# Reordering the fixed cycle of a fused attention and two-layer kernel: probabilities ahead of the scores, input matmuls in halves

## The chip, the cores and the metric

The kernel runs on one core of one Trainium2 chip. The metric is the device time of one execution in microseconds (us). Before the change three runs took 1663.9, 1669.32 and 1674.0 us, so the median is 1669.32 us. Every reading of the trace below comes from one profiled execution of 1669.26 us.

## The reference

Three stages follow each other. Attention with a top-32 mask comes first: 4 batches, 8 heads, 576 positions, head width 64. Its 2304 tokens of width 512 then go through two layers with 2048 hidden units each, the first with a rational function between its two products, the second with h cos(h).

```python
scores = scale * np.matmul(q, k.transpose(0, 1, 3, 2))
kth = np.partition(scores, -top_k, axis=-1)[..., -top_k:-top_k + 1]
scores = np.where(scores >= kth, scores, -1000000000.0)
attn = softmax(scores); x = attn @ v            # -> (2304, 512)
h = x @ w_in                                    # first layer
g = (a0 + a1*h + a2*h**2 + a3*h**3) / (1 + |b0|*|h| + |b1|*h**2 + 1e-6)
x = g @ w_out
h = x @ w_in2; g = h * cos(h); out = g @ w_out2 # second layer
```

## The kernel before

The three stages run as one pipeline. Its step is called a unit here; the loop at the end of `body` counts it as `u` and passes it to the functions as `i`. In unit i attention works on 128 query positions of a pair of heads: `topk` finds the 32 greatest scores of tile i, `av(i - 1)` transposes the probabilities of tile i-1 and multiplies them with V, and `qk(i + 1)` computes the scores of tile i+1. Beside it one group of 256 hidden units of each layer, for a block of 256 tokens, goes through its steps: the first layer runs 9 units behind attention (`UA`), the second 18 units (`UB`). There are 72 attention tiles, so a unit past 72 holds work of the layers alone.

Every fp32 product of the layers is made of three products of fp32r halves (a high and a low part). `mm_in` therefore issues 24 matmuls of 256 columns for one group (2 blocks of hidden units, 4 chunks of the width, 3 products) into one bank of PSUM, `out1` another 24, and `out2` 12 of 512 columns.

Units 20 to 71 (`U0`, `U1`) run in a fixed cycle. The function `unit` writes the order of the cycle by hand: the wrapper `InOrder` ties each instruction to the one written before it on the same engine, so VectorE (DVE), ScalarE (ACT), GpSimd (POOL) and TensorE (PE) each follow the order of `unit`. SyncE's queue, which starts the streamed loads, is placed by the framework. Outside those units `events` places the work of the layers, and the framework may reorder it.

The order of TensorE in one unit before the change is: nine transposes of the probabilities (tiles `pp..a`, `pp..b`, and one into `sx`), the scores of the first head (four matmuls into `sx`), all 24 matmuls of `in1`, the scores of the second head, the probabilities times V (18 matmuls into `sx`), 24 of `in2`, 12 of `out2`, 24 of `out1`.

ScalarE follows with: three copies of the transposes (`pt`), the copy `sS` of the first head's scores, the high part `gg` of the first layer, in every second unit a table load and the sine, then `w`, `r`, `q`, `u` of `in1`, the copy `sS` of the second head's scores, the copy `xs` of the attention output, in every second unit a table load, the high part `gg` of the second layer, `nb` and the two exponentials `e`, two steps `r` of the reciprocal, `hs`, `rr`, `n` of `in2`, and the high part `q` of a later query tile.

PSUM has eight banks. The tag `h` has two, which pass in turn to `pp..a`, `pp..b`, `h` of `in1`, (in every fourth unit `bc` of the normalisation) and `h` of `in2`. The tile `sx` has two, shared by the scores (columns 0 to 287 of both banks), one transpose and the attention output (columns 288 to 415 of one bank each). `y` and `o` have two each. The streamed low parts of the weights go through four buffers of the tag `st`, with five loads in each unit.

Of the kernel before, what the change touches and what calls it, by code (L numbers as in the profile page):

```python
# [36 lines left out]
NG = NF // 2  # L37
SINB = 2
UA, UB = 9, 18
# [76 lines left out]
def body(tc, out, qt, kt, vt, ident_d, w1_d, w1o_d, a_d, b_d, w2_d, w2o_d):  # L116
# [5 lines left out]
    with ExitStack() as ctx:  # L122
# [27 lines left out]
        nu = len(units)  # L150
# [35 lines left out]
        def high_q(i):  # L186
            if 8 <= i < nu:
                qs_[i][1] = x = att.tile([P, 2, 2, P], F32R, tag="q", bufs=QB, name=f"q{i}")
                A.activation(x[:, 0], qs_[i][0], AF.Copy)
# [287 lines left out]
        def mm_in(m, k, g):  # L477
            h = ps_h.tile([P, 2, BT], F32, tag="h", name=f"h{m}_{k}_{g}")
            xh, xl = xhl[k] if m == 0 else x2hl[k]
            lo = lot.pop((m, k, g)).rearrange("p f (c t) -> p f c t", t=P)  # L480
            for i in range(2):
                f = 2 * g + i
                for c in range(NCC):
                    wh = whi[m][:, c, f * P:(f + 1) * P]
                    PE.matmul(h[:, i, :], wh, xh[:, c, :], start=(c == 0), stop=False)
                    PE.matmul(h[:, i, :], wh, xl[:, c, :], start=False, stop=False)
                    PE.matmul(h[:, i, :], lo[:, i, c, :], xh[:, c, :], start=False, stop=(c == NCC - 1))
            return h

        g1, ys, x2hl = {}, {}, {}  # L490

        def in1(k, g):
            h = mm_in(0, k, g).rearrange("p a t -> p (a t)")
            w, q, r, u = (mo.tile([P, BT * 2], F32, tag="m1" + t, bufs=NU if t == "u" else N1, name=f"{t}{k}_{g}") for t in "wqru")
            A.activation(w, h, AF.Copy)
            A.activation(r, w, AF.Abs)
            A.activation(q, r, AF.Identity, scale=b1, bias=b0)
            A.activation(u, w, AF.Identity, scale=na3, bias=na2)
            g1[k, g] = (q, r, u, w)

        def pol1(k, g):
            q, r, u, w = g1[k, g]
# [43 lines left out]
        def x2high(k):  # L546
            x2hl[k] = [late[0].tile([P, NCC, BT], F32R, tag=t, name=f"{t}{k}") for t in ("x2h", "x2l")]
            for c in range(2):
                cs = slice(2 * c, 2 * c + 2)
                A.activation(x2hl[k][0][:, cs], ys[k][:, cs], AF.Copy)  # L550
# [6 lines left out]
        rt, rp, os_, g2 = {}, {}, {}, {}  # L557

        def in2(k, g):
            g2[k, g] = mm_in(1, k, g).rearrange("p a t -> p (a t)")  # L560

        def phase2(k, g):
            h = g2.pop((k, g))
            if g % SINB == 0:
                rp[k, g // SINB] = late[0].tile([P, SINB, 512], F32, tag="rr", bufs=2, name=f"rr{k}_{g}")
            rs = rp[k, g // SINB]
            rr = rs[:, g % SINB]
            hs = late[0].tile([P, 512], F32, tag="hs", bufs=N2, name=f"hs{k}_{g}")
            A.activation(hs, h, AF.Copy)
            n = late[0].tile([P, DM], F32, tag="n", bufs=OBB, name=f"n{k}_{g}")  # L570
            if k >= DV2:
                V.tensor_scalar(rr, hs, 1.0 / TWO_PI, 0.25, op0=ALU.mult, op1=ALU.add)
            else:
                A.activation(rr, hs, AF.Identity, scale=1.0 / TWO_PI, bias=quarter)
            A.activation(n, rr, AF.Identity, bias=magic)
            rt[k, g] = rr, hs, n
# [45 lines left out]
        def store(k, t):  # L622
            o, parts = os_[k], qts[2 * k + t]
            n = P // len(parts)
            if k == NB - 1:
                if t == 0:
                    rt["ob"] = late[0].tile([P, SINB, DM], F32, tag="rr", bufs=2, name=f"ob{k}")
                ob = rt["ob"][:, t]
                A.activation(ob[:, :DM // 2], o[:, t, :DM // 2], AF.Copy)
                V.tensor_copy(ob[:, DM // 2:], o[:, t, DM // 2:])  # L630
            else:
                ob = late[0].tile([P, DM], F32, tag="ob", bufs=OBB, name=f"ob{k}_{t}")
                A.activation(ob, o[:, t, :], AF.Copy)
            for c, (b, tt) in enumerate(parts):
                row = b * S + tt * P
                (SP if c == 0 else A).dma_start(out=out[row:row + n, :], in_=ob[c * n:(c + 1) * n, :])
# [12 lines left out]

        flat = []  # L650
        for u in range(UB + NB * NG + 3):
            for f, d in ((in1, UA), (in2, UB), (out2, UB + 3), (out1, UA + 1)):
                if 0 <= u - d < NB * NG:
                    flat.append((f, *divmod(u - d, NG)))
        loads = []
# [38 lines left out]
        def ev(x, *fs):  # L694
            if 0 <= x < NB * NG:
                for f in fs:
                    run_event((f, *divmod(x, NG)))

        def last(x):
            return 0 <= x < NB * NG and x % NG == NG - 1  # L700
# [6 lines left out]
        nrm, low, held, x2, ob = [], [], [], [], []  # L707
# [51 lines left out]
        def events(u, p):  # L759
            if p == 0:  # L760
                ev(u - UA - 1, *((mid1,) if u <= U0 else (mid1, end1)))
                ev(u - UB - 1, mid2, sin2, table)
            if p == 1:
                for k in x2:
                    x2low(k)
                for k, t in ob:
                    store(k, t)
                x2.clear()
                ob.clear()
                if u > U0:  # L770
                    ev(u - UB - 3, low2)
                    ev(u - UA - 1, low1)
                ev(u - UB - 2, mul2, high2)
                ev(u - UA, in1, pol1, rec1)
            if p == 2:
                if u < U0:
                    ev(u - UA - 1, end1, low1)
                ev(u - UB, in2, phase2)
            if p == 3:
                ev(u - UB - 3, out2)  # L780
                if last(u - UB - 3):
                    store((u - UB - 3) // NG, 0)
                    store((u - UB - 3) // NG, 1)
            if p == 4:
                ev(u - UA - 1, out1)
                if last(u - UA - 1):
                    x2high((u - UA - 1) // NG)
                    x2.append((u - UA - 1) // NG)

        def unit(i, prev):  # L790
            t = topk(i)
            next(t)
            next(prev)
            next(prev)
            for x in low:
                next(x, None)
            low.clear()
            a = av(i - 1)
            next(a)
            nq = qk(i + 1) if i + 1 < nu else iter(())  # L800
            next(nq, None)
            ev(i - UA - 1, mid1, end1)
            low_q(i + 2, V)
            if i % 4 == 0:
                nrm.append(norm((i - 1) // 8, (i - 1) // 4 % 2))
                next(nrm[-1])
            ev(i - UB - 1, mid2)
            for k in x2:
                x2low(k)
            x2.clear()  # L810
            ev(i - UB - 3, low2)
            ev(i - UA - 1, low1)
            for k, h in ob:
                store(k, h)
            ob.clear()
            ev(i - UB - 1, sin2)
            ev(i - UB - 2, mul2)
            ev(i - UA, in1, pol1)
            next(nq, None)
            if i + 2 < nu:  # L820
                load_k(i + 2)
            load_q(i + 4)
            if i % 4 == 0:
                next(nrm[-1])
            next(a, None)
            load_v(i)
            if i % 4 == 0:
                next(nrm[-1])
            ev(i - UB - 1, table)
            ev(i - UB - 2, high2)  # L830
            ev(i - UB, in2)
            ev(i - UB - 3, out2)
            ev(i - UA - 1, out1)
            for _ in range(4):
                next(t)
            ev(i - UA, rec1)
            ev(i - UB, phase2)
            high_q(i + 3)
            if i % 8 == 0:
                for x in nrm:  # L840
                    next(x)
                low.extend(nrm)
                nrm.clear()
            if last(i - UA - 1):
                x2high((i - UA - 1) // NG)
                x2.append((i - UA - 1) // NG)
            if last(i - UB - 3):
                store((i - UB - 3) // NG, 0)
                ob.append(((i - UB - 3) // NG, 1))
            for x, a in held:  # L850
                store_k(x, *a)
            held[:] = [(prep(*a), a) for a in preps.get(i, [])]
            return t
# [64 lines left out]
```

## Time and profile before

| what | value |
|---|---|
| median of three runs | 1669.32 us |
| profiled execution | 1669.26 us, its span 1667.5 us |
| PE busy | 1339.2 us (80%) |
| DVE busy | 1204.0 us (72%) |
| ACT busy | 1114.5 us (67%) |
| POOL busy | 587.2 us (35%) |
| mean granted clock of PE | 0.886 |

The span is the time from the first to the last instruction in the trace, and the execution's own time holds what lies around it. Busy shares are means over stages with different limits. PE's busy time counts matmuls that overlap in the array, so it does not say how many more could be done. A granted clock of 1.00 is 2.4 GHz, 0.50 is 1.2 GHz. Nearly all instructions are recorded under line 80, the wrapper's call, so groups are read by their tiles' names.

### The profile page before, as it was taken

The page shows a single profiled execution, that of the slowest core. Times are in us where ns is not written, and L with a number is a line of the kernel's source. Part 1 is how long each engine was busy: PE and PEld are TensorE (multiplying, and loading weights), DVE is VectorE, ACT ScalarE, POOL GpSimd, SP SyncE. Part 2 cuts the span into 40 slices and gives each one's busy share as a digit, 9 for nine tenths or more (in the row PEclk, how much of TensorE's full clock was granted, in tenths as well). Part 3 has the DMA queues.
Part 4 walks back from the last instruction along what each step waited for, and adds up shares of the span by engine and source line. Part 5 has one row for each costly group of instructions (what it writes and reads, how often), then busy time and mean ns, then how long its engine had stood idle before and what let it go on. Part 6 is the DMA issues. An engine that isn't in the chain of part 4 may idle for free.

```text
span 1667.5 us, 25031 instructions
## 1 busy us (share of the span) xinstructions
PE 1339.2 (80%) x8944; PEld 1181.9 (71%) x8944; DVE 1204.0 (72%) x2514; ACT 1114.5 (67%) x1918; POOL 587.2 (35%) x434
## 2 busy tenths in 40 slices
PE   6776866677878888788878887888887888899998
PEld 3344655577777777777777777777777777789986
DVE  7989978897767766767777677676776576746643
ACT  7787778566676666666666666666666665668753
POOL 3665555323333333333333333333333333332000
PEclk9677887788898989889898999898988898899999
DMA  8977688523455544444555544444445555556776
GB/s 272 324 239 239 210 260 290 167 80 130 162 176 174 185 163 150 145 154 162 166 176 189 169 155 155 167 154 145 151 161 175 190 200 201 187 184 228 244 253 223
DMA packets 155948, 314.98 MB, mean 189 GB/s; under 512 B 12592, under 2 KB 47536, under 8 KB 155824
## 3 DMA queue, kind: packets, MB, share of 16 engines
q1 hardware_dynamic: 122832, 261.99, 46.7%
q10 hardware_dynamic: 32992, 51.39, 9.6%
q8 instruction: 71, 1.16, 0.3%
q14 instruction: 53, 0.43, 0.1%
HBM read 278.20 MB, written 35.13 MB: 188 GB/s over the span
## 4 chain that ended last, share of the span: by engine, by line
PE 47%; ACT 23%; DVE 15%; DMA 6%; issue 4%; ACTq 2%; POOL 2%; SPq 0%; POOLq 0%; DVEq 0%
PE h L80 18%; PE sx L80 10%; PE o L80 9%; PE y L80 8%; DVE e L80 6%; DVE hd L80 4%; ACT sS L80 3%; ACT r L80 3%; ACT rr L80 2%; ACTq L80 2%; ACT L80 2%; ACT u L80 2%; DVE cb L80 2%; ACT e L80 2%; ACT w L80 2%
## 5 line engine op out<-in xcount | busy, mean ns | idle before, releaser
L80 DVE MAX8 hd<-e 128x8 f32<-128x288 f32 (+1 forms) x576 | 320.6, 596 | 0.0
L80 DVE TENSOR_TENSOR e<-sS 128x576 f32<-128x576 f32 x144 | 169.9, 1219 | 158.1 <-ACT sS L80 148.0
L80 DVE MATCH_REPLACE8 e<-hd,e 128x288 f32<-128x288 f32 (+1 forms) x432 | 230.9, 541 | 0.0
L80 PE MATMUL y<-gg,w1o 128*128 128x256 f32 x1152 | 217.1, 287 | 11.5 <-DVE x2l L80 6.6
L80 POOL TENSOR_TENSOR gg<-rr,gg 128x512 fp32r<-128x512 f32 x56 | 73.2, 1308 | 418.4 <-DVE rr L80 314.7
L80 DVE SCALAR_TENSOR_TENSOR e<-sS,hd,e 128x576 f32<-128x576 f32 x144 | 122.1, 877 | 131.8 <-ACT e L80 131.8
L80 PE MATMUL o<-w2o,gg 128*128 128x512 f32 x864 | 211.2, 392 | 3.3 <-DMA w2o<-w2o 3.2
L80 PEld LDWEIGHTS y<-gg,w1o 128*128 128x128 f32 x1152 | 186.8, 194 | 19.6 <-ACT gg L80 10.9
L80 PE MATMUL h<-x2h,w2hi 128*128 128x256 f32 x576 | 196.8, 342 | 0.5 <-ACT hs L80 0.5
L80 PE MATMUL h<-x2l,w2hi 128*128 128x256 f32 x576 | 186.4, 324 | 0.0
L80 PE MATMUL h<-x2h,lo 128*128 128x256 f32 x576 | 184.2, 320 | 1.4 <-DMA lo<-w2lo 1.4
L80 PEld LDWEIGHTS o<-w2o,gg 128*128 128x128 f32 x864 | 157.1, 188 | 35.5 <-DMA w2o<-w2o 4.9
L80 PE MATMUL h<-xh,w1hi 128*128 128x256 f32 x576 | 167.9, 291 | 0.8 <-ACT pt17a L80 0.3
L80 PE MATMUL h<-xl,w1hi 128*128 128x256 f32 x576 | 166.3, 289 | 0.0
L80 PE MATMUL h<-xh,lo 128*128 128x256 f32 x576 | 166.2, 289 | 0.0
L80 PE MATMUL y<-gg,w1ol 128*128 128x256 f32 x576 | 164.2, 285 | 0.2 <-DMA w1ol<-w1ol 0.2
L80 PE MATMUL sx<-k,q 128*128 128x288 f32 (+1 forms) x576 | 108.2, 316 | 55.5 <-ACT xs L80 10.3
L80 POOL TENSOR_TENSOR gg<-u,gg 128x512 fp32r<-128x512 f32 x64 | 83.8, 1309 | 191.1 <-ACT gg L80 191.1
L80 PEld LDWEIGHTS h<-x2h,w2hi 128*128 128x128 f32 x576 | 137.0, 238 | 15.9 <-issue 14.2
L80 PEld LDWEIGHTS h<-x2l,w2hi 128*128 128x128 f32 x576 | 137.2, 238 | 0.2
L80 PEld LDWEIGHTS h<-x2h,lo 128*128 128x128 f32 x576 | 134.8, 234 | 2.1 <-DMA lo<-w2lo 2.0
L80 PEld LDWEIGHTS sx<-k,q 128*128 128x128 f32 (+1 forms) x576 | 83.9, 190 | 71.0 <-ACT xs L80 11.5
(1023 smaller groups left out, 3456.5 us busy)
## 6 DMA issues: line engine op xcount, KB each, us to landing
w2o<-w2o SPq DMA_DIRECT2D x144, 512.0 KB, 4.5
lo<-w1lo SPq DMA_DIRECT2D x72, 512.0 KB, 3.7
w1ol<-w1ol SPq DMA_DIRECT2D x72, 512.0 KB, 3.7
lo<-w2lo SPq DMA_DIRECT2D x72, 512.0 KB, 4.5
k<-kdr ACTq DMA_DIRECT2D x44, 576.0 KB, 4.9
raw<-w SPq DMA_DIRECT2D x32, 512.0 KB, 5.1
v<-vt ACTq DMA_DIRECT2D x48, 320.0 KB, 3.1
qr<-qt ACTq DMA_DIRECT2D x72, 128.0 KB, 3.7
```

Of the source, the lines that this page charges most:

```text
L80: r = f(*a, **k)
```

## The change

The change rewrites the order inside `unit`, with the same instructions and the same tiles. It has these parts.

- `mm_in` issues 12 of its 24 matmuls at once and returns a function for the other 12; `in1` and `in2` become `in1`/`in1b` and `in2`/`in2b`.
- TensorE's order becomes: transposes, first half of `in1`, probabilities times V, second half of `in1`, scores of the first head, first half of `in2`, scores of the second head, second half of `in2`, `out1`, `out2`.
- ScalarE's order becomes: `pt` three times, `gg` of the first layer, sine, `xs`, `w`, `r`, `sS` of the first head, `q`, `u`, `sS` of the second head, the issues of the loads of k, q and v, table load, `gg` of the second layer, and the rest as before.
- `out1` goes before `out2` everywhere, also in the list from which the streamed loads are issued and in `events`.
- The rest of a normalisation that lay ahead of `mid1` and `end1` on VectorE goes behind them; both stores of a finished output block move into the unit after it.

```diff
-            for i in range(2):
+
+            def half(i):
                 f = 2 * g + i
                 for c in range(NCC):
...
-            return h
+
+            half(0)
+            return h.rearrange("p a t -> p (a t)"), half
...
-            for f, d in ((in1, UA), (in2, UB), (out2, UB + 3), (out1, UA + 1)):
+            for f, d in ((in1, UA), (in2, UB), (out1, UA + 1), (out2, UB + 3)):
...
         def unit(i, prev):
             t = topk(i)
             next(t)
             next(prev)
             next(prev)
+            a = av(i - 1)
+            next(a)
+            ev(i - UA - 1, mid1, end1)
             for x in low:
                 next(x, None)
             low.clear()
-            a = av(i - 1)
-            next(a)
-            nq = qk(i + 1) if i + 1 < nu else iter(())
-            next(nq, None)
-            ev(i - UA - 1, mid1, end1)
...
-            for k, h in ob:
-                store(k, h)
+            for k in ob:
+                store(k, 0)
+            ev(i - UB - 1, sin2)
+            ev(i - UA, in1)
+            next(a, None)
+            if i % 4 == 0:
+                next(nrm[-1])
+            ev(i - UB - 2, mul2)
+            if i % 4 == 0:
+                next(nrm[-1])
+            ev(i - UA, in1b, copy1)
+            nq = qk(i + 1) if i + 1 < nu else iter(())
+            next(nq, None)
+            ev(i - UA, lin1, pol1)
+            ev(i - UB, in2)
+            next(nq, None)
+            ev(i - UB, in2b)
+            for k in ob:
+                store(k, 1)
             ob.clear()
-            ev(i - UB - 1, sin2)
-            ev(i - UB - 2, mul2)
-            ev(i - UA, in1, pol1)
-            next(nq, None)
             if i + 2 < nu:
                 load_k(i + 2)
             load_q(i + 4)
-            if i % 4 == 0:
-                next(nrm[-1])
-            next(a, None)
             load_v(i)
-            if i % 4 == 0:
-                next(nrm[-1])
+            ev(i - UA - 1, out1)
+            ev(i - UB - 3, out2)
             ev(i - UB - 1, table)
             ev(i - UB - 2, high2)
-            ev(i - UB, in2)
-            ev(i - UB - 3, out2)
-            ev(i - UA - 1, out1)
             for _ in range(4):
                 next(t)
             ev(i - UA, rec1)
-            ev(i - UB, phase2)
-            high_q(i + 3)
...
+            ev(i - UB, phase2)
+            high_q(i + 3)
```

## Rows read from the trace of the kernel before

**Rows 1.** Two stages: busy time of each engine, granted clock, DMA share, GB/s.
```profile
800.00:900.00 100.00, 79.94 (x543) 72.97 (x543) 68.45 (x144) 69.25 (x116) 37.22 (x28) 0.88 0.50 164
...
1500.00:1600.00 100.00, 99.78 (x734) 95.14 (x733) 60.91 (x92) 74.69 (x108) 10.02 (x8) 1.00 0.70 233
```

**Rows 2.** Tiles pt19a and pt71a: first transpose copy of units 20 and 72, start time.
```profile
L80 ACT ACTIVATE pt19a<-pp19a x1: 597/597/597, 367.8 to 367.8; 128x512 f32<-128x512 f32 x1
...
L80 ACT ACTIVATE pt71a<-pp71a x1: 599/599/599, 1489.4 to 1489.4; 128x512 f32<-128x512 f32 x1
```

**Rows 3.** Waits, 400 to 1300 us: total us, times, longest.
```profile
PE sx L80 <- ACT sS L80: 134.6, 42, 3.7
```

**Rows 4.** Timeline of PE, one unit: start, us, operation, count, idle before.
```profile
816.60 0.60 PE L80 MATMUL pp40a<-ident,e 128*128 128x128 f32 x4
...
818.54 0.80 PE L80 MATMUL sx<-k,q 128*128 128x288 f32 x4 [0.80 <-ACT pt40t L80]
819.18 0.28 PE L80 MATMUL h<-xh,w1hi 128*128 128x256 f32 x1
...
822.05 0.70 PE L80 MATMUL sx<-k,q 128*128 128x288 f32 x4
825.65 0.80 PE L80 MATMUL sx<-pt40t,v 128*128 128x128 f32 x2 [2.90 <-ACT sS L80]
...
828.28 0.58 PE L80 MATMUL h<-x2h,w2hi 128*128 128x256 f32 x1
...
833.00 2.89 PE L80 MATMUL o<-w2o,gg 128*128 128x512 f32 x12
835.73 0.40 PE L80 MATMUL y<-gg,w1o 128*128 128x256 f32 x2
```

**Rows 5.** The same columns as rows 1, two stretches of this unit.
```profile
818.50:822.70 4.20, 4.16 (x32) 3.97 (x32) 4.17 (x10) 1.74 (x3) 0.66 (x1) 1.00 0.73 235
825.60:828.20 2.60, 2.55 (x18) 2.08 (x18) 2.60 (x7) 0.00 (x0) 2.60 (x3) 0.50 0.60 213
```

**Rows 6.** Timeline of ACT in the same unit.
```profile
817.23 0.60 ACT L80 ACTIVATE pt40a<-pp40a 128x512 f32<-128x512 f32 x1 [0.33 <-PE pp40a L80]
...
818.20 0.28 ACT L80 ACTIVATE pt40t<-sx 128x128 f32<-128x128 f32 x1
...
822.25 0.60 ACT L80 ACTIVATE w<-h 128x512 f32<-128x512 f32 x1 [0.65 <-PE h L80]
...
824.97 0.63 ACT L80 ACTIVATE sS<-sx 128x576 f32<-128x576 f32 x1
...
828.57 0.62 ACT L80 ACTIVATE gg<-rr 128x512 fp32r<-128x512 f32 x1
...
833.20 0.60 ACT L80 ACTIVATE hs<-h 128x512 f32<-128x512 f32 x1 [1.16 <-PE h L80]
...
835.22 0.40 ACT L80 ACTIVATE q<-qr 128x256 fp32r<-128x256 f32 x1
```

**Rows 7.** Timeline of PE ahead of the fixed cycle: probabilities times V, first and last.
```profile
199.86 0.38 PE L80 MATMUL sx<-pt10t,v 128*128 128x128 f32 x2
...
201.00 0.27 PE L80 MATMUL sx<-pt10b,v 128*64 128x128 f32 x1
```

**Rows 8.** Groups of ACT, 400 to 1300 us: count, busy us, mean ns, idle before.
```profile
L80 ACT ACT_TABLE_LOAD x42 | 53.9, 1283 | 3.0 <-issue 1.3
...
L80 ACT ACTIVATE rr<-rr 128x1024 f32<-128x1024 f32 x21 | 22.2, 1059 | 0.2
...
L80 ACT ACTIVATE xh<-xs 128x512 fp32r<-128x512 f32 x10 | 5.7, 616 | 0.0
```

**Rows 9.** Timeline of PE in a unit of two batches: scores of one head.
```profile
1380.06 1.32 PE L80 MATMUL sx<-k,q 128*128 128x288 f32 x8 [0.80 <-ACT pt66t L80]
```

**Rows 10.** Timeline of DVE: the first two steps of a top-32 search.
```profile
848.72 2.50 DVE L80 TENSOR_TENSOR e<-sS 128x576 f32<-128x576 f32 x2 [0.27 <-ACT sS L80]
```

**Rows 11.** DMA issues of the page: KB each, median us from issue to landing.
```profile
lo<-w1lo SPq DMA_DIRECT2D x72, 512.0 KB, 3.7
```

More of the change, by code (lines that the diff above doesn't have):

```diff
@@ L487, in mm_in, with in1b, copy1 @@
                     PE.matmul(h[:, i, :], lo[:, i, c, :], xh[:, c, :], start=False, stop=(c == NCC - 1))
-            return h
+            half(0)
+            return h.rearrange("p a t -> p (a t)"), half
         g1, ys, x2hl = {}, {}, {}
         def in1(k, g):
-            h = mm_in(0, k, g).rearrange("p a t -> p (a t)")
+            g1[k, g] = mm_in(0, k, g)
+        def in1b(k, g):
+            g1[k, g][1](1)
+        def copy1(k, g):
+            h, _ = g1[k, g]
             w, q, r, u = (mo.tile([P, BT * 2], F32, tag="m1" + t, bufs=NU if t == "u" else N1, name=f"{t}{k}_{g}") for t in "wqru")
@@ L496, in in1, with lin1 @@
             A.activation(r, w, AF.Abs)
+            g1[k, g] = (q, r, u, w)
+        def lin1(k, g):
+            q, r, u, w = g1[k, g]
             A.activation(q, r, AF.Identity, scale=b1, bias=b0)
             A.activation(u, w, AF.Identity, scale=na3, bias=na2)
-            g1[k, g] = (q, r, u, w)
         def pol1(k, g):
@@ L559, in in2, with in2b @@
         def in2(k, g):
-            g2[k, g] = mm_in(1, k, g).rearrange("p a t -> p (a t)")
+            g2[k, g] = mm_in(1, k, g)
+        def in2b(k, g):
+            g2[k, g][1](1)
         def phase2(k, g):
-            h = g2.pop((k, g))
+            h, _ = g2.pop((k, g))
             if g % SINB == 0:
@@ L765, in events @@
                     x2low(k)
-                for k, t in ob:
-                    store(k, t)
+                for k in ob:
+                    store(k, 0)
+                    store(k, 1)
                 x2.clear()
@@ L773, in events @@
                 ev(u - UB - 2, mul2, high2)
-                ev(u - UA, in1, pol1, rec1)
+                ev(u - UA, in1, in1b, copy1, lin1, pol1, rec1)
             if p == 2:
@@ L777, in events @@
                     ev(u - UA - 1, end1, low1)
-                ev(u - UB, in2, phase2)
+                ev(u - UB, in2, in2b, phase2)
             if p == 3:
+                ev(u - UA - 1, out1)
+                if last(u - UA - 1):
+                    x2high((u - UA - 1) // NG)
+                    x2.append((u - UA - 1) // NG)
+            if p == 4:
                 ev(u - UB - 3, out2)
@@ L783, in events @@
                     store((u - UB - 3) // NG, 1)
[L784 to L788, printed above, removed]
         def unit(i, prev):
@@ L812, in unit @@
             ev(i - UA - 1, low1)
-            for k, h in ob:
-                store(k, h)
+            for k in ob:
+                store(k, 0)
+            ev(i - UB - 1, sin2)
[13 more added lines that the diff above has]
+            ev(i - UB, in2b)
+            for k in ob:
+                store(k, 1)
             ob.clear()
-            ev(i - UB - 1, sin2)
-            ev(i - UB - 2, mul2)
-            ev(i - UA, in1, pol1)
-            next(nq, None)
             if i + 2 < nu:
@@ L847, in unit @@
             if last(i - UB - 3):
-                store((i - UB - 3) // NG, 0)
-                ob.append(((i - UB - 3) // NG, 1))
+                ob.append((i - UB - 3) // NG)
             for x, a in held:
```

## The prediction

> **What bounds the kernel now.** I read the views in this order: the stages, the length of a unit, the waits, then one unit on each engine. In the middle of the run no engine is full: PE 80%, ACT 69%, DVE 68%, POOL 37%, and PE's granted clock is 0.88 [rows 1]. The 52 units of the fixed cycle take from the first transpose copy of unit 20 to that of unit 72, 1489.4 - 367.8 = 1121.6 us, or 21.57 us each [rows 2]. That is two thirds of the span, and the change concerns almost nothing else.
>
> What sets the 21.57 us is seen on PE [rows 4]. Transposes at 816.60, a wait of 0.80 for the third copy, scores of the first head at 818.54 (0.64 long), 24 matmuls of `in1` from 819.18 to 822.05 (2.87), scores of the second head, and then 2.90 of nothing: the product with V waits for ACT's copy `sS`, which stands behind `w`, `r`, `q` and `u` and ends at 824.97 + 0.63 = 825.60 [rows 6]. The two write and read different columns of the same bank, and the product starts 0.05 after the copy. This wait is there in each of the 42 units between 400 and 1300 us, 3.2 us on the mean [rows 3]. Afterwards the clock is 0.50, where it was 1.00 before [rows 5]: the product with V takes 828.28 - 825.65 = 2.63 instead of 201.00 + 0.27 - 199.86 = 1.41 [rows 7], and `in2` takes 833.00 - 828.28 = 4.72 instead of 2.87. `out2` takes 2.73, and `out1`, with as many matmuls of the same size as `in1`, 2.87. The sum is 22.0 for this unit: a chain through PE and ACT in turn, not one busy engine.
>
> **The change, part by part.** I count from the first transpose of a unit.
>
> *PE.* The first copy `pt` ends at 817.23 + 0.60 - 816.60 = 1.23 [rows 4, 6]; only then is its bank free for `in1`, so the first half runs from 1.29 to 2.73 (half of 2.87). Under it ACT makes the other copies, the last of which ends at 1.88, so the 0.80 of waiting goes and the product with V follows at 2.73, at full clock until 4.14. Second half of `in1` to 5.58, scores 6.22, half of `in2` 7.66, scores 8.30, half of `in2` 9.74, `out1` 12.61, `out2` 15.34. So PE alone needs 15.34 us for a unit.
>
> *ACT.* After the copies `gg` ends at about 2.50. In every second unit a table load (1.28) and the sine (1.06) follow [rows 8], to 4.84, then `xs` to 5.1. The first scores need the bank that `xs` reads, and they come at 5.58: covered by 0.5. `w` starts 0.20 after the second half of `in1`, as 822.25 after 822.05 before, at 5.78. From `w` to `sS` it was 2.72; one more copy of 0.63 now lies between, so the second `sS` runs from 9.13 to 9.76. The second scores wait for the first `sS`, which ends at 7.67 against 7.66 on PE: just covered, with nothing to spare. From `gg` to the end of the high part `q` it was 835.62 - 828.57 less a wait of 1.16, thus 5.89 [rows 6]: ACT is done at 15.65. The next copy `pt` can't start before 15.34 + 0.63 = 15.97. So a unit without a sine is PE's, 15.34; in one with the sine the table load of 1.28 lies in that tail, ACT ends at 16.93, and the next unit starts 0.95 late.
>
> *Eight units* (one block of 256 tokens) then cost 8 x 15.34 = 122.7; 4 x 0.95 = 3.8 for the units with the sine; 2 x 0.7 for the two normalisations (one copy of some 0.62 and four transposes each); 1.2 for the two copies `xh` of 0.616 [rows 8]; 0.9 for the two copies of the block's new input beyond the slack of 0.32; about 0.7 for the kraw copies, which fall into some units only; 0.5 for the issues of k, q and v, which now stand between `sS` and the table load. Those five are estimates from that row. Sum 131.2, or 16.4 a unit, and 853 for 52. In the last eight units two batches share a tile, and the scores of a head take 1.32 instead of 0.64 [rows 9]; that adds 8 x 2 x 0.68 = 10.9. Total 864, a gain of 258.
>
> *What I cost at nothing.* DVE needs 68.45% of 21.57 = 14.8 a unit, POOL 8.0 [rows 1]; both stay under 16.4, and the 14.8 has in it that the first two steps of the search take 2.50 where POOL works beside them [rows 10]. The low part `xl`, now behind `mid1` and `end1`, is wanted by `in1` in one unit of eight; uncovered it would cost at most such a pair, 2.5/8 = 0.3 a unit. `out1` now wants its low part from POOL at 9.74 and not some 19 us into the unit; it is second in POOL's order, behind work that starts before 2.5. The streamed loads: four buffers and five loads, so the low part of the next `in1` can be fetched only when `in2` has given up its buffer, at 9.74. It takes 3.7 [rows 11] and is wanted at 16.6: 3.2 to spare. SyncE's queue issues these in order; the nearest in front waits for `out2`'s buffers, which come free earlier. A unit moves 164 GB/s x 21.57 = 3.54 MB, at 16.4 us 216 GB/s, and the stage from 1500 us on moves 233 with PE at 99.78% [rows 1].
>
> *Not shown before:* the clock in the new order. At best it is 1.00 throughout, as I count; at worst all runs like the stretch after the wait (priced below). I take 1.00, because the wait of 0.80 left 1.00 behind it [rows 4, 5] and the waits I forecast are of that size. Outside the fixed cycle only the order of `out1` and `out2` and of two stores changes. The stage from 1500 us shows PE full, so there is nothing to gain; a wait of 0.80 in each of some 40 units would lose 32. I take 0.
>
> *A rule that speaks against the change.* The shortest wait of rows 4 left the clock at 1.00 and the longest brought it to 0.50 [rows 5]. The Trainium skill ("TensorE: Matmul & The Clock Gate", section "A second HAM failure mode: psum-queue depth-cycling") tells of a kernel that passed PSUM buffers on between groups of matmuls and whose clock swung between the two levels for it. The new order has more such joints, since it cuts both input groups in halves. By that rule the time would be that of the rival on the clock below. The row of 0.80 disagrees so far.
>
> **The sum.** The profiled execution took 1669.26, of which the span is 1667.5; the median of the runs is 1669.32, so nothing has to be converted. 1669.3 - 258 = 1411.
>
> **Rivals.**
> *ACT becomes the chain.* It works 69.25% of 21.57 = 14.9 a unit [rows 1]. In the new order it must stand still between `gg` (2.50) and `xs` (about 4.2), and between `xs` (4.5) and `w` (5.78): 3.0. If no unit can hide that, a unit is 17.9, the 52 are 942 with the two-batch scores, and the time is 1489. For it: the sine units are already ACT's. Against: the sine fills most of the 3.0 there, and in the others PE ends later.
> *The wait comes back elsewhere*, so that the change does not do what it says: the scores wait for `xs` and then `sS`, where I have 0.5 and 0.0 to spare. With the whole 3.2 [rows 3] back, a unit is 19.6, the time 1578. Against: half a group of matmuls lies under each copy.
> *The loads.* If the memory gave no more than its 164 GB/s, the unit would stay at 21.57 and the time at 1669; at 200 it is 17.7, and the time 1478. Against: 233 is shown.
> *Slower: the clock stays at half.* Then each group of 24 matmuls costs 4.72 - 2.87 = 1.85 more, four times with `out2` (as many columns), and the product with V 1.22: 8.6 a unit, which makes 25.0 and 1858 us. It turns the sign from 58% of that on (21.4 - 16.4 = 5.0 of 8.6), that is when `in2`, `out1` and `out2` run low as well. For it: PE waits at more places. Against: rows 4 and 5, and after the wait of 2.90 the clock came back within `in2`.
> *Better:* PE hides all of ACT: 52 x 15.34 + 11 = 809, time 1356.
>
> **How the numbers follow.** The forecast has 0.62, ACT's chain 0.20, the returning wait 0.05, the loads 0.06 (0.01 of it without any gain), the clock 0.05, the better case 0.02. The forecast's own band is 1375 (two thirds of the 1.06 a unit that ACT adds to PE are hidden) to 1450 (0.75 a unit more from the loads or the clock). ACT's chain and the loads at 200 GB/s take the range up to 1500; above it lie the returning wait, the slowest loads and the clock, some 0.12, and below it the better case. A measurement of this kernel can tell about 0.5% from no change. Faster than that: 0.62 + 0.20 + 0.05 + 0.05 + 0.02, rounded to 0.93 with a little taken off for mishaps; within it 0.02; slower 0.05.
>
> **What the profile after would show.** Right: the first transpose copies of units 20 and 72 some 864 apart; PE's wait for `sS` in front of the product with V gone; granted clock near 1.00 in the middle, `in2` in two halves of 1.44; ACT without a wait before `pt` in units with a sine, and with waits before `xs` and `w` in the others; PE over 93% busy. Wrong: a wait of over 1 us in front of the scores or of `out1` in most units; the clock at 0.50 for `in2` or the product with V; SP's queue holding back `lo`; DVE without a gap, its search ending after ACT is ready for `nb`. A time over 1500 would say that a chain which I hold for covered sets the unit.

## The result and the profile after

The changed kernel takes 1453.09 us (median of 4 runs, 1448.5 to 1454.1) against 1667.53 for the kernel before in the same measurement: a ratio of 0.871, 95% interval 0.867 to 0.874. The forecast was 1411 with a range of 1375 to 1500. The gain is 214 where 258 were forecast.

The first line of the page, with busy time and share of the span for each engine, and the stage from 800 to 900 us (columns as in rows 1):

```profile
PE 1272.2 (88%) x8944; PEld 1121.2 (77%) x8944; DVE 1200.8 (83%) x2514; ACT 1100.5 (76%) x1918; POOL 585.1 (40%) x434
```
```profile
800.00:900.00 100.00, 95.39 (x709) 87.33 (x708) 88.41 (x190) 80.14 (x139) 43.39 (x32) 0.95 0.62 203
```

Compared with [rows 1], every engine does the same work in less time: PE is at 95% where it was at 80%, and it takes 709 matmuls in these 100 us instead of 543. The first transpose copies of units 20 and 72 after the change:

```profile
L80 ACT ACTIVATE pt19a<-pp19a x1: 597/597/597, 370.6 to 370.6; 128x512 f32<-128x512 f32 x1
...
L80 ACT ACTIVATE pt71a<-pp71a x1: 598/598/598, 1265.5 to 1265.5; 128x512 f32<-128x512 f32 x1
```

The 52 units take 1265.5 - 370.6 = 894.9 instead of 1121.6 [rows 2], or 17.21 each. The forecast had 864. So 226.7 were won in the cycle; 2.8 were lost ahead of unit 20 and 8.7 behind unit 72 (186.8 instead of 178.1 to the end of the span).

Units are not alike. The length of a unit is taken from its first transpose copy on ACT to that of the next unit. The transposes of tile 48 belong to unit 49, since a unit transposes the tile before its own. Here is PE from the last group of unit 48, through unit 49, to the first matmul of `in1` in unit 50 (columns as in rows 4), with the first row of the groups:

```profile
861.29 2.92 PE L80 MATMUL o<-w2o,gg 128*128 128x512 f32 x12
864.05 0.60 PE L80 MATMUL pp48a<-ident,e 128*128 128x128 f32 x4
865.27 0.65 PE L80 MATMUL pp48b<-ident,e 128*128 128x128 f32 x4 [0.62 <-ACT hs L80]
...
867.57 0.47 PE L80 MATMUL h<-xh,w1hi 128*128 128x256 f32 x1 [1.53 <-ACT pt48a L80]
...
870.19 0.63 PE L80 MATMUL sx<-pt48t,v 128*128 128x128 f32 x2
...
871.94 0.39 PE L80 MATMUL h<-xh,w1hi 128*128 128x256 f32 x1
...
873.46 0.70 PE L80 MATMUL sx<-k,q 128*128 128x288 f32 x4
...
875.52 0.80 PE L80 MATMUL sx<-k,q 128*128 128x288 f32 x4
...
880.47 2.91 PE L80 MATMUL o<-w2o,gg 128*128 128x512 f32 x12
883.22 0.60 PE L80 MATMUL pp49a<-ident,e 128*128 128x128 f32 x4
...
884.59 0.39 PE L80 MATMUL h<-xh,w1hi 128*128 128x256 f32 x1 [0.22 <-ACT pt49a L80]
```

The 2.90 in front of the product with V [rows 4] is gone, and no wait of PE for `sS` is left in the cycle: the product follows the first half of `in1` without a gap, the scores stand 2.06 apart with half of `in2` between them. What is left is a wait at the start of the unit behind one with a sine, here unit 49: 0.62 for `hs` inside the transposes and 1.53 for the copy `pt`, in front of the first half of `in1`. Behind it the matmuls of `in1` start 0.215 apart and not 0.12: this half takes 870.19 - 867.57 = 2.62, not 1.44, and the product with V 1.75, not 1.41. Two units without a sine, 49 and 51, each from 0.6 us ahead of its first transpose copy (columns as in rows 1):

```profile
866.30:883.30 17.00, 15.73 (x111) 14.67 (x112) 14.96 (x33) 12.14 (x24) 6.87 (x5) 0.90 0.41 144
899.90:915.30 15.40, 14.18 (x111) 13.22 (x112) 14.77 (x32) 11.88 (x23) 6.90 (x5) 1.00 0.53 175
```

PE has the same work in both. Unit 51, with a wait of 1.23 for the copy `pt`, keeps a granted clock of 1.00 and takes 15.4: the forecast's 15.34. Unit 49 has a clock of 0.90 and takes 17.0. Of the twenty units without a sine from 23 to 61, ten are of the one kind (15.45 on the mean) and ten of the other (16.95). None of the twenty units with a sine from 22 to 60 has a low clock, and they take 17.43 on the mean, where the forecast's terms (with its estimates for normalisation, `xh` and kraw) make 17.1.

ACT in a unit with a sine, ahead of its tail; ACTq is the sequencer that issues:

```profile
857.32 0.33 ACTq L80 DMA_DIRECT2D k<-kdr  x1
857.61 0.63 ACT L80 ACTIVATE sS<-sx 128x576 f32<-128x576 f32 x1
857.69 0.55 ACTq L80 DMA_DIRECT2D qr<-qt  x1
858.28 0.61 ACTq L80 DMA_DIRECT2D v<-vt  x1
858.92 1.28 ACT L80 ACT_TABLE_LOAD   x1 [0.67 <-issue]
```

The second `sS` ends at 857.61 + 0.63 = 858.24, but the table load behind it starts at 858.92, when the sequencer has issued the third load. The waits of ACT over the 52 units:

```profile
ACT xs L80 <- PE sx L80: 71.0, 28, 4.1
ACT w L80 <- PE h L80: 53.8, 52, 1.8
ACT L80 <- issue: 23.5, 26, 2.5
ACT gg L80 <- issue: 5.1, 3, 2.2
```

The first two were forecast (ACT stands before `xs` in units without a sine, and before `w` in all). In the last two ACT stands idle until its sequencer has issued the loads. They are 28.6 together, and were priced at 0.5 in eight units, 3 in all.

### The profile page after: what moved, and what is told of

Same layout as the page of the kernel before. It is cut to its first block, busy times and chain, and to the rows that moved or that the text cites. A ratio compares the mean times of both kernels' runs of the same rounds, so it can differ in the third digit from the quotient of the medians.

```text
span 1452.3 us, 25010 instructions
## 1 busy us (share of the span) xinstructions
PE 1272.2 (88%) x8944; PEld 1121.2 (77%) x8944; DVE 1200.8 (83%) x2514; ACT 1100.5 (76%) x1918; POOL 585.1 (40%) x434
## 4 chain that ended last, share of the span: by engine, by line
PE 45%; ACT 20%; DMA 3%; issue 3%; DVE 2%; ACTq 2%; POOL 1%; SPq 0%
PE h L80 22%; PE sx L80 9%; PE y L80 7%; PE o L80 6%; ACT r L80 4%; ACT e L80 3%; ACTq L80 2%; ACT q L80 2%; ACT rr L80 2%; DMA lo<-w2lo 1%; ACT n L80 1%; ACT gg L80 1%; DMA w2o<-w2o 1%; ACT sS L80 1%; DVE e L80 1%
## 5 line engine op out<-in xcount | busy, mean ns | idle before, releaser
L80 PE MATMUL h<-xh,w1hi 128*128 128x256 f32 x576 | 183.2, 318 | 47.9 <-ACT pt24a L80 2.1
L80 PE MATMUL h<-xh,lo 128*128 128x256 f32 x576 | 171.4, 298 | 0.9 <-DMA lo<-w1lo 0.9
L80 PEld LDWEIGHTS h<-xh,w1hi 128*128 128x128 f32 x576 | 117.7, 204 | 68.8 <-issue 7.1
L80 PE MATMUL h<-x2h,lo 128*128 128x256 f32 x576 | 164.0, 285 | 3.0 <-DMA lo<-w2lo 3.0
L80 PE MATMUL h<-x2h,w2hi 128*128 128x256 f32 x576 | 163.5, 284 | 0.5 <-ACT hs L80 0.5
L80 PE MATMUL h<-x2l,w2hi 128*128 128x256 f32 x576 | 163.6, 284 | 0.1
L80 POOL TENSOR_TENSOR q<-q,r 128x512 f32<-128x512 f32 x64 | 86.2, 1347 | 133.3 <-ACT q L80 133.3
L80 POOL TENSOR_TENSOR cb<-cb,raw 128x512 int32<-128x512 int32 x64 | 92.8, 1454 | 73.2 <-DVE cb L80 59.6
L80 PEld LDWEIGHTS h<-xh,lo 128*128 128x128 f32 x576 | 118.5, 206 | 1.4 <-DMA lo<-w1lo 1.4
L80 PEld LDWEIGHTS h<-xl,w1hi 128*128 128x128 f32 x576 | 118.4, 206 | 1.0 <-issue 0.7
```

The lines of the kernel that those rows point to most:

```text
L80: r = f(*a, **k)
```

## The experiments

The kernel before took 1670.1 to 1671.0 in the measurements that follow, each time on the same chip and together with the run; the ratios are to it, with 95% intervals. Differences "to the change" are to its 1453. Units are counted as above.

**e1: the three loads issued later.** Edit of the changed kernel:

```diff
-            if i + 2 < nu:
-                load_k(i + 2)
-            load_q(i + 4)
-            load_v(i)
             ev(i - UA - 1, out1)
...
             for _ in range(4):
                 next(t)
+            if i + 2 < nu:
+                load_k(i + 2)
+            load_q(i + 4)
+            load_v(i)
             ev(i - UA, rec1)
```

> The changed kernel with the issues of the k, q and v loads moved on ACT's queue from ahead of the table load to behind the two exponentials. Theory A (the change cost more than forecast because ACT stands idle behind these issues in the units with a sine, 23.5 + 5.1 us in the 52 units, and because the wait on PE that follows brings the clock to half): the idle time marked issue goes, the units with a sine become 0.7 to 0.9 shorter, the time falls from 1453 to 1425-1435. Rival B (DVE, busy 88 to 93%, sets the unit through the search): no change, 1453 within 5. Rival C (transfers of k and v are what is late): they are issued 2.5 to 4 us later, PE waits for DMA k or v, 1460 or more.

Measured: 1447.0, ratio to before 0.865 (0.862 to 0.868), against 0.871 (0.867 to 0.874) for the change. The 6 us under the change lie within the two intervals. Two rows of its waits tell why theory A's number was missed:

```profile
ACT r L80 <- issue: 12.9, 24, 1.9
...
PE sx L80 <- DMA v<-vt: 12.1, 16, 2.7
```

Of the 28.6 of idle time, 12.9 stays, now behind the exponentials, and PE waits for v. Both A and C were at work; B was not, since the units with a sine did become shorter (17.06 on the mean instead of 17.43). Of the twenty units without a sine only four have a low clock, but with the waits for v they still take 16.16 on the mean, after 16.20.

**e8: k and q later, v as in the change.**

```diff
-            if i + 2 < nu:
-                load_k(i + 2)
-            load_q(i + 4)
             load_v(i)
...
             for _ in range(4):
                 next(t)
+            if i + 2 < nu:
+                load_k(i + 2)
+            load_q(i + 4)
             ev(i - UA, rec1)
```

> As e1_loads_late, but the load of v stays ahead of the table load, and only k and q go behind the exponentials. Theory (e1 lost with v, which PE waited for 12 us in all, what it won on ACT): no wait of PE for DMA v, the idle time marked issue under 8 in the 52 units, 1453 falls to 1430-1438. Rival (the issue time is paid in either place): 1445 to 1453.

Measured: 1414.9, ratio 0.847 (0.844 to 0.850), 38 less than the change. ACT in one of its units with a sine, and its wait for issues over the 52 units:

```profile
868.64 0.34 ACTq L80 DMA_DIRECT2D v<-vt  x1
869.05 0.63 ACT L80 ACTIVATE sS<-sx 128x576 f32<-128x576 f32 x1
869.69 1.28 ACT L80 ACT_TABLE_LOAD   x1
...
871.75 0.78 ACT L80 ACTIVATE e<-sS,nb 128x576 f32<-128x576 f32 x1
871.75 0.33 ACTq L80 DMA_DIRECT2D k<-kdr  x1
872.12 0.56 ACTq L80 DMA_DIRECT2D qr<-qt  x1
872.43 0.76 ACT L80 ACTIVATE e<-sS,nb 128x576 f32<-128x576 f32 x1
873.10 0.71 ACT L80 ACTIVATE r<-q,qc 128x512 f32<-128x512 f32 x1
```
```profile
ACT L80 <- issue: 1.1, 4, 0.3
```

The issue of v (0.34) ends before `sS` does, those of k and q lie under the exponentials, and the table load follows at once. No wait of PE for v shows. The gain is larger than the 28.6 - 1.1 = 27.5 of idle time taken away, and the time lies below the 1430 to 1438 expected: the units with a sine fall from 17.43 to 16.72 on the mean, and those without from 16.20 to 15.52, where only one of twenty is left with a low clock. The 52 units take 856.5, 7.5 under the forecast of 864.

**e6: work of PE behind the transposes.** `out2` issues six of its twelve matmuls and returns the rest, which the next unit issues behind its transposes:

```diff
...
             a = av(i - 1)
             next(a)
+            ev(i - UB - 4, out2b)
             ev(i - UA - 1, mid1, end1)
...
```

> The changed kernel with the second six of the 12 matmuls of out2 behind the transposes of the next unit, 1.37 us of PE work in front of the first half of in1. Theory (in the units behind one with a sine, PE's wait of 1.2 to 2.1 for the first transpose copy brings the clock to half, which costs 1.6 in some 20 units): the wait shrinks below 0.8, the clock is 1.00 in all units from 21 to 62, odd units take 15.4 to 15.6; 1453 falls to 1425-1435. Rival (the wait moves in front of the transposes, which need e and hs, and the clock falls all the same): 1453 within 6 or slower.

Measured: 1430.8, ratio 0.857 (0.855 to 0.860), 22 less than the change. PE around the transposes of tile 48, in unit 49:

```profile
847.95 0.63 PE L80 MATMUL pp48a<-ident,e 128*128 128x128 f32 x4
850.46 0.66 PE L80 MATMUL pp48b<-ident,e 128*128 128x128 f32 x4 [1.88 <-ACT hs L80]
...
850.98 1.63 PE L80 MATMUL o<-w2o,gg 128*128 128x512 f32 x6
852.76 0.39 PE L80 MATMUL h<-xh,w1hi 128*128 128x256 f32 x1 [0.15 <-ACT pt48a L80]
```

The wait did move inside the transposes, to 1.88, as the rival said, but here the clock did not fall with it: only two of the twenty units without a sine have a low clock. Six matmuls of `out2` now cross the border between units, so units are compared in pairs: one with a sine and one without take 17.72 + 15.03 = 32.75 on the mean, after 33.63. ACT's idle time for issues is unchanged (23.6 and 5.0). PE's waits of over 0.15 us in units 20 to 63 fall only from 42.7 to 37.2 in all. Eight fewer units with a low clock, at 16.95 - 15.45 = 1.5 each, are 12 of the 22; so most of the gain is the clock and the smaller part the waits themselves.

**e9: both.**

> Both repairs together: the loads of k and q behind the exponentials (e8, 1414.9) and six matmuls of out2 behind the transposes (e6, 1430.8). Theory (two costs: the issues on ACT's queue, and the half clock behind PE's wait, which e8 has already removed in all but two units): only a little is left for the second repair, where ACT's tail still ends late in units with a sine: 1400 to 1413. Rival (the two gains add, since they are different waits: 22 and 38 from 1453): 1390 or less. Rival 2 (the half of out2 behind the transposes delays gg on ACT and eats its gain): 1414 to 1425.

Measured: 1403.3, ratio 0.839 (0.838 to 0.841). The gains (38 and 22) don't add: they share the low clock, which had already gone in all but one of the twenty units in e8, as the theory had it. This is the fastest of the kernels tried, 50 under the change.

**e2: no table loads in the cycle.** In units 20 to 71 the sine becomes a copy and the reload of the table is left out:

```diff
-                A.activation(rs, rs, AF.Sin, scale=-SSC)
+                A.activation(rs, rs, AF.Copy if C0 <= A.piece < C1 else AF.Sin, scale=-SSC)
...
-            if g % SINB == SINB - 1 and k < NB - 1:
+            if g % SINB == SINB - 1 and k < NB - 1 and not C0 <= A.piece < C1:
```

> The changed kernel without table loads in units 20 to 71; the sine there is replaced by a scaled copy of the same tile, so this part of the computation is left out. Theory A: ACT's tail in the even units is 1.3 shorter and its head too, every unit becomes PE's with 15.4 to 15.6, the granted clock is 1.00 in all of them, 52 units take 815-830 instead of 895, the time is 1370-1390. Rival B (DVE sets it): DVE's 15.1 busy us a unit and its waits stay, units of 16.5 and more, 1420 or more.

Measured: 1405.7, and 844.7 for the 52 units. The direction is A's: the clock is 1.00 in all units from 22 to 62, and those without a sine take 15.5 on the mean, so ACT's table loads in the sine units are what made the others slow. Units where the sine is left out still take 16.24 on the mean, above the 15.4 to 15.6 expected. DVE (rival B) is not the bound. The time is 16 above the range expected, which left out the normalisations (16.8 to 17.5 in one unit of eight) and the two-batch units (143.5 for the last eight); neither goes with the sine.

**e3: undivided input products.** `mm_in` issues all 24 matmuls, `in1b` and `in2b` nothing.

```diff
             half(0)
+            half(1)
             return h.rearrange("p a t -> p (a t)"), half
...
```

> The changed kernel with the two input products undivided: transposes, 24 matmuls of in1, product with V, scores, 24 of in2, scores, out1, out2; the copies on ACT keep their order. Theory (the halves cover the copies xs and sS): the first scores wait some 0.4 for xs, the second scores end at 10.2 instead of 8.3, so the second sS and ACT's tail come 1.2 later in every unit; 1.0 to 1.5 a unit more, and more low clock: 1510 to 1560. Rival (only the place of the product with V matters, the halves do nothing): 1453 within 7.

Measured: 1525.9, ratio 0.913 (0.910 to 0.916): 73 more than the change, within the 1510 to 1560 expected. Waits from 400 to 1200 us, PE and ACT:

```profile
PE sx L80 <- ACT xs L80: 12.5, 33, 0.4
```
```profile
ACT sS L80 <- PE sx L80: 48.6, 45, 1.9
```

The scores wait 0.38 for `xs`, and the second `sS` waits for its scores, 1.1 on the mean; after the change the same wait came to 2.7 in total over the 52 units.

**e4: q and u ahead of the first sS.**

```diff
-            ev(i - UA, in1b, copy1)
+            ev(i - UA, in1b, copy1, lin1)
             nq = qk(i + 1) if i + 1 < nu else iter(())
             next(nq, None)
-            ev(i - UA, lin1, pol1)
+            ev(i - UA, pol1)
```

> The changed kernel with q and u back ahead of the first sS on ACT. Theory (the second scores wait for the first sS, covered to 0.0): the second scores wait 1.4 in each unit, at least 52 x 1.4 = 74 more, 1527, and up to 1600 if the clock falls behind that wait. Rival (ACT's order does not matter as long as in2's half lies under the copies): 1453 within 7.

Measured: 1518.3, ratio 0.909 (0.905 to 0.912): 65 more than the change, against at least 74 expected. The second scores wait as forecast (waits from 400 to 1200 us):

```profile
PE sx L80 <- ACT sS L80: 63.6, 44, 1.5
```

That is 1.45 a unit, or 75 in 52 units, where the cycle became 66 longer (961.2). The rest has two parts: only seven of the twenty units without a sine have a low clock here, after ten, which gives back some 4.5, and the last eight units, where the scores of two batches take longer, grew by 6.3 and not by 8 x 1.45 = 11.6. PE's waits for the copies `pt` stayed (34.8 in units 20 to 63, after 36.0).

**e11: the order alone**, the edits of e3 and e4 together.

> The changed kernel with both e3 and e4: the input products undivided, and q and u ahead of the first sS on ACT; of the change only the place of the product with V (and of out1) is left. Theory: with all of in2 between the two scores, 2.87 us lie over the first sS, so the place of q and u costs nothing here, and ACT's wait of 1.21 for the second scores in e3 takes them up: the time is that of e3, 1526 within 8. The place of the copies is then worth 65 only together with the halves. Rival (the two costs add, 73 + 65): 1580 to 1600.

Measured: 1537.2, ratio 0.920 (0.913 to 0.927), 11 above e3: outside the theory's 8 by a little, and far from the rival's 1580. Of the gain of 214, the new order of TensorE alone therefore brings 133 (1670.1 - 1537.2). This kernel also holds the moved stores and the moved rest of a normalisation; those were not tried alone. With the product with V ahead of the scores the four kernels are

| | q, u late (as in the change) | q, u first (as before) |
|---|---|---|
| input products in halves | 1453 | 1518 |
| undivided | 1526 | 1537 |

so the halves alone bring 19 and the copies alone 11 (which lies within the two intervals), but both together 84: each needs the other's cover.

**p1: one copy moved in the kernel before.** `in1` is split so that `q` and `u` follow the second `sS`; TensorE's order stays as before.

```diff
...
-            ev(i - UA, in1, pol1)
+            ev(i - UA, in1)
             next(nq, None)
+            ev(i - UA, lin1, pol1)
```

> The kernel before with one part of the change alone: on ACT the second sS ahead of q and u. Theory: PE's wait of 3.2 in front of the product with V falls by the 1.43 of q and u; with the clock still at half behind it a unit is 20.1 (time 1593), with the clock kept 17.5 (1460). I expect the clock to be kept in most units: 1470 to 1530. Rival (something else than ACT's copy holds the product back): 1667 within 10.

Measured: 1533.2, ratio 0.918 (0.915 to 0.921). One wait of PE from 400 to 1200 us:

```profile
PE sx L80 <- ACT sS L80: 70.7, 42, 2.4
```

The wait falls from 3.2 [rows 3] to 1.68 a unit. Units without a sine then take 17.5 at a clock of 1.00, as calculated; those with a sine 19.6 to 20.2 at 0.91 to 0.92, and so the time lies just above the 1470 to 1530 expected. Beside the change's 214, 138 (1671.0 - 1533.2) can be had by moving one copy in the old order.

**e5: out2 ahead of out1** again in the unit and in the list of loads:

```diff
...
-            ev(i - UA - 1, out1)
-            ev(i - UB - 3, out2)
+            ev(i - UB - 3, out2)
+            ev(i - UA - 1, out1)
```

> The changed kernel with out2 ahead of out1 again, in the unit, in the list of loads and outside the fixed cycle. Theory: inside the cycle the order of the two costs nothing (both find their inputs ready), so the 52 units stay at 895 within 5; the 8.7 by which the stage behind unit 72 became longer (178.1 before, 186.8 after) comes from this swap and goes: 1444. Rival: out1 early is what PE's order needs, 52 units over 910. Rival 2: the stage behind unit 72 is longer for another reason (the stores): 1453 within 4.

Measured: 1455.3, ratio 0.871 (0.868 to 0.874), the 52 units 899.5: no difference that this can tell, so the order of the two is worth nothing inside the cycle. The stage behind unit 72 took 185.1, not shorter; but the edit left the order in `events` as the change has it, so it did not test what the expectation said of that stage.

**e10: e8 with out2 and its stores first outside the cycle.** In `events`, out2 and the stores go to the step ahead of out1, and the list of loads has that order outside units 20 to 71.

> e8 with out2 and its stores ahead of out1 outside the fixed cycle, as before the change; in e5 the order of the functions outside the cycle was left as the change has it. Theory (this order makes the stage behind unit 72 8.7 longer: 178.1 before, 186.8 after): that stage falls below 181, the time from 1414.9 to 1405-1410. Rival (it is the state in which the cycle leaves the loads, not that order): the stage stays at 185 or more, 1412 to 1418.

Measured: 1409.3, ratio 0.844 (0.843 to 0.846). The stage behind unit 72 took 184.4 where e8 has 185.6: the swap is not what made it longer. The time lies in the theory's 1405 to 1410 all the same, but not for its reason, and its interval overlaps that of e8 (0.844 to 0.850). In the changed kernel's trace that stage has a wait of PE for a streamed load that is longer than any of the kind before (1.4), and a stretch at a lower clock further on:

```profile
PE h L80 <- DMA lo<-w2lo: 3.0, 1, 3.0
```
```profile
1386.00:1416.00 30.00, 26.59 (x160) 24.32 (x159) 9.45 (x16) 12.15 (x17) 0.00 (x0) 0.89 0.65 209
```

In e10 the longest wait of that kind is 1.5, and the stage is still 6.3 longer than the 178.1 before, so this wait can be a part of the 8.7 at most. The rest was not tried.

## Why the prediction was right

*What bounded the kernel*: right. The chain through PE and ACT set the unit; p1 moved one copy in it, and the time fell by 138.

*PE's sum of 15.34*: right. Units without a sine at full clock take 15.4 in the changed kernel, and 15.44 on the mean in e8.

*ACT's table load as the second bound*: right. e8 has 16.72 for the units with a sine and 17.1 was forecast; without the table loads (e2) they take 16.24, and the clock stays at 1.00 from unit 21 to unit 64.

*The cover with 0.0 to spare under the first `sS`*: right, and it is that narrow: e4 took it away and the wait of 1.45 came back at once. The rival of the returning wait did not occur: PE has no wait for `sS` left in the cycle.

*The mis-sized term: "0.5 for the issues of k, q and v"* in eight units. The step was the estimate that these issues cost almost nothing where they now stand. No row stands behind the 0.5: [rows 8], to which the prediction points for its five estimates, has no issue. In the cycle the issues cost 28.6 of idle time, 4.4 in eight units, and with the waits and the low clock behind them some 38 in all, 5.9 in eight units: that is e8 against the change. The miss in the cycle is 894.9 - 864 = 31, and it is smaller than this one term because the cycle without it (856.5 in e8) came out 7.5 under the forecast; that the rest of the sum was too high was luck. The other 11 of the miss lie outside the cycle.

The place of the issues mattered. In the trace of the kernel before, an issue took about as long, but lay under `q` and `u` (here that of q, in unit 41), and ACT's idle time for issues over the 52 units was 3.7:

```profile
823.54 0.81 ACT L80 ACTIVATE q<-r,babs 128x512 f32<-128x512 f32 x1
823.61 0.56 ACTq L80 DMA_DIRECT2D qr<-qt  x1
```
```profile
ACT L80 <- issue: 3.7, 12, 0.6
```

In the new order they stand in front of the tail, where ACT is what the unit waits for. The forecast's 3 is about what they cost at their old place.

*"I take 1.00" for the clock*: only half right. A wait of 0.80 left the clock alone [rows 4, 5], but those that came were of 1.2 to 2.1. Of the units without a sine from 23 to 61, six had a wait of up to 1.34 for the copy `pt`, and it fell in none; fourteen had one of 1.5 or more, and it fell in ten. Ten units with 1.5 more are 15 of the 31 lost in the cycle, and the stage from 800 to 900 us has 0.95, where a clock near 1.00 was forecast. e6, which keeps the issues and removes most of the low clock, gains 22. These 22 are no third cost: in e8 the low clock went with the issues, and most of the waits became shorter (0.7 to 1.5, two of 2.1).

The rule of the Trainium skill named in the prediction ("TensorE: Matmul & The Clock Gate", "A second HAM failure mode: psum-queue depth-cycling") was nearer than the forecast's 1.00 in that ten waits for a PSUM buffer were followed by a low clock, and far from the rival built on it: the mean clock over the span rose from 0.886 to 0.922.

*ACT becomes the chain* (1489): not as a whole; ACT does set the units with a sine. *The loads*: 199 to 217 GB/s were reached in the stages from 400 to 1100 us of the cycle without a wait in most units; v was late only when it was issued later (e1). *Slower by the clock*: its price of 1.85 for 24 matmuls makes 0.93 for 12, and unit 49 shows 2.62 - 1.44 = 1.18 for the 12 of one half, but in ten units only. The price was too low because the 4.72 of `in2` [rows 4] holds six matmuls at full clock at its end: the granted clock over it is 0.58, not 0.50.

*Left over*: 2.8 ahead of unit 20 and 8.7 behind unit 72. Their cause stays open.

## What to carry to other kernels

When two engines pass a unit back and forth, count the path through both in the new order and look for covers that come out at zero: each must be tested, since here taking one away cost 65. An instruction that only issues a transfer is work of its engine too; put it under a long instruction of an engine that isn't late, and not ahead of the stretch that the others wait for. A price for a wait is not complete without the clock behind it: at one place here a wait of 1.2 us left the clock alone, while one of 1.5 us was followed by a stretch at a lower clock that cost 1.6 us more. No limit follows from that, since four waits as long or longer left it alone.

## What the runs showed that was not expected

In the rows above the issue of one load occupies ACT's sequencer for 0.33 to 0.61 us, and three in a row held back an instruction that was ready by 0.67. The Trainium skill ("DMA: Bandwidth & Descriptors", section "Issuing engines are not separate DMA queues") calls this time usually small beside the transfer. The trace agrees with that (3.9 to 6.2 from issue to landing here), but beside ACT's own instructions of 0.6 it is not small.

The length of a wait alone does not decide the clock. After the change, units 43 and 47 have the same wait at the same place, and only the second loses clock behind it (PE, then the two units, columns as in rows 1):

```profile
765.43 0.39 PE L80 MATMUL h<-xh,w1hi 128*128 128x256 f32 x1 [1.85 <-ACT pt42a L80]
```
```profile
832.53 0.39 PE L80 MATMUL h<-xh,w1hi 128*128 128x256 f32 x1 [1.85 <-ACT pt46a L80]
```
```profile
764.80:780.20 15.40, 14.77 (x116) 13.81 (x117) 14.19 (x31) 11.29 (x22) 8.55 (x6) 1.00 0.66 215
831.90:848.90 17.00, 16.37 (x117) 15.15 (x118) 14.26 (x31) 11.32 (x23) 8.52 (x6) 0.90 0.57 183
```

In e6 it is the same: a wait of 1.88 between two groups of transposes left unit 49 at 1.00, and one of 1.89 at that place went with 0.92 in unit 41. What else decides was not separated.
